# Scatters of the last routing group made independent, and a slot's row load moved behind two weight pieces

## The chip, the cores and the metric

The kernel runs on one core of one Trainium2 chip. The metric is device time in microseconds (us) of one execution. A profile records one execution; its span runs from the first to the last instruction.

## The reference, cut to what matters

Three layers follow each other: a gated linear attention over 4 x 8 heads of 768 steps, a dense feed-forward layer with softplus (3072 tokens, 384 -> 2048 -> 384), and a mixture of eight experts with one expert for each token. The change touches the way from the second to the third layer and the third layer:

```python
def _moe2_ref(x, modality_id, w_gate, modality_bias, w1, w2):
    logits = x @ w_gate + modality_bias[modality_id]
    e_idx = np.argmax(logits, axis=1)
    ...
    gate_w = probs[np.arange(N), e_idx]
    for e in range(E):
        mask = e_idx == e
        h = np.maximum(x[mask] @ w1[e], 0.0)
        out[mask] = gate_w[mask, None] * (h @ w2[e])
```

Here N is 3072, D is 384, E is 8 and the hidden width of an expert is 1024.

## The kernel before, in words

Names used below: PE is TensorE's matmul, ACT is ScalarE, DVE is VectorE, POOL is GpSimd and SP is SyncE, on whose queue nearly all loads are issued.

**Routing.** The 3072 tokens are eight groups of 384. When the feed-forward layer has finished a group, `route1` takes its outputs out of PSUM and `route2` computes each token's expert and its place among that expert's rows (`pos`). Three indirect DMAs from POOL (L492), 128 tokens each, then scatter the rows into `xs`, a buffer in DRAM sorted by expert. A row is 388 floats: 384 values, the gate weight, the token's number and two zeros. All three write the one tensor `xs`, so each waits until the one before has landed. Before the last group's scatters, `pad_rows` (L828, eight DMAs from SP) fills the places behind each expert's rows.

**Slots.** The third layer works in slots: up to 256 rows of one expert (a pair slot) or 128 rows (a single). There are 16: slots 0 to 2 are planned before the last group is routed, their rows are loaded early, and slots 3 to 15 after it (`plan_rest`); slots 3 to 11 are pair slots, slots 12 to 15 are singles. A slot's work is

- `m_load` (L702): SP reads the row offset from the plan (`roff`) and issues one DMA `xr <- xs` (L705). There are three `xr` buffers, so the rows of slot x+1 go into the buffer of slot x-2, whose last reader is the output scatter of slot x-2 (it takes the token numbers from `xr`). That load also waits for the scatters into `xs`.
- `m_weights` (L708): SP reads the expert's number (`woff`); eight pieces of 384 KB follow, w1 and w2 by turns. I number them p0 to p7, so p0, p2, p4, p6 are w1 and p1, p3, p5, p7 are w2. A piece goes into one of six `raw` buffers (L724), ACT rounds it to the high part (L725) and DVE takes the remainder as the low part (L726), which frees the `raw` buffer. In singles w1 goes straight into place (L721). The split weights have two sets of buffers, by turns of slots.
- `m_T` (L730): PE turns the rows (L746, in two steps, four and two transposes), ACT and DVE split them into `thl` (L748, L749). The two steps share one PSUM buffer.
- `m_up` (L751): eight steps of 9 matmuls from `thl` and w1 (L764), each followed by relu on ACT (L766) and a remainder on DVE (L767).
- `m_down` (L780): 24 matmuls for each 128 rows (L787), scaling on ACT into `o` (L791), and an indirect DMA from POOL that scatters the result rows to `out` (L792). All of these write `out`, so each waits until the one before has landed.

**Order.** `m_slots` (L803) runs slot x, and at its start calls `m_fetch` for slot x+1, which before the change calls `m_load` first and `m_weights` after it; the eight pieces are then issued one for each step of `m_up`, and `m_T` of slot x+1 follows step 6. An engine executes its own queue strictly in order. The order within a queue is set when the kernel is built, by a planner that starts from the order of the program and from the dependencies and may move instructions of an engine past each other.

Of the kernel before, what the change touches and what calls it, by code (L numbers as in the profile page):

```python
# [20 lines left out]
TG = 384  # L21
NG = NT // TG
# [3 lines left out]
SLOT = 256  # L26
# [16 lines left out]
RW = 388  # L43
# [7 lines left out]
def moe_chain(ctx, tc, qT, kT, fT, vp, w_in, w_out, mod, w_gate, mbias, w1, w2, out):  # L51
    nc = tc.nc
# [15 lines left out]
    xs = dp.tile([E * CAP + SLOT, RW], F32, name="xs")  # L68
# [173 lines left out]
    padt = cp.tile([128, RW], F32, name="padt")  # L242
# [190 lines left out]
            del gst[s]  # L433


    rt = {}

    def sm(nm, shape, dt=F32):
        return gp.tile(shape, dt, tag=nm, name=nm)
# [12 lines left out]
    def route2(G):  # L452
        d = rt[G]
        lg, rows = d["lg"], d["rows"]
        mx = sm("mx", [128, 3])
        oh = sm("oh", [128, 3, 8])
        sc = sm("sc", [128, 3, 8])
        ohb = sm("ohb", [128, 3, 8], BF16)
        m2 = sm("m2", [128, 3])
        bc = lambda t: t.unsqueeze(2).to_broadcast([128, 3, 8])  # L460
        nc.vector.tensor_reduce(mx, lg, axis=AX.X, op=ALU.max)
        nc.vector.tensor_tensor(oh, lg, bc(mx), op=ALU.is_equal)
        nc.vector.tensor_tensor(sc, oh, wt8.unsqueeze(1).to_broadcast([128, 3, 8]), op=ALU.mult)
        nc.vector.tensor_reduce(m2, sc, axis=AX.X, op=ALU.max)
        nc.vector.tensor_scalar(m2, m2, 1.0, None, op0=ALU.max)
        nc.vector.tensor_tensor(oh, sc, bc(m2), op=ALU.is_equal)
        nc.vector.tensor_copy(ohb, oh)
        p = ps_r.tile([128, 512], F32, tag="r", name="r")
        for j in range(3):
            pj = p[:, 8 * j:8 * j + 8]  # L470
            nc.tensor.matmul(pj, onesb, runb, start=True, stop=False)
            for i in range(j):
                nc.tensor.matmul(pj, onesb, ohb[:, i, :], start=False, stop=False)
            nc.tensor.matmul(pj, ustr, ohb[:, j, :], start=False, stop=True)
        for j in range(3):
            nc.vector.tensor_tensor(run, run, oh[:, j, :], op=ALU.add)
        nc.vector.tensor_copy(runb, run)
        nc.vector.tensor_tensor(sc, p[:, 0:24].rearrange("p (j e) -> p j e", j=3),
                                base.unsqueeze(1).to_broadcast([128, 3, 8]), op=ALU.add)
        nc.vector.tensor_tensor(sc, sc, oh, op=ALU.mult)  # L480
        nc.vector.tensor_reduce(m2, sc, axis=AX.X, op=ALU.add)
        pos = sm("pos", [128, 3], I32)
        nc.vector.tensor_scalar(pos, m2, BIG, None, op0=ALU.add)
        nc.vector.tensor_tensor(lg, lg, bc(mx), op=ALU.subtract)
        nc.scalar.activation(lg, lg, AF.Exp)
        nc.vector.tensor_copy(rows.bitcast(I32)[:, :, 385], ids[:, 3 * G:3 * G + 3])
        nc.vector.memset(rows[:, :, 386:388], 0.0)
        nc.vector.tensor_reduce(mx, lg, axis=AX.X, op=ALU.add)
        nc.vector.tensor_scalar(mx, mx, 1e-9, None, op0=ALU.add)
        nc.vector.reciprocal(rows[:, :, 384], mx)  # L490
        for j in range(3):
            nc.gpsimd.indirect_dma_start(  # L492
                out=xs, out_offset=bass.IndirectOffsetOnAxis(ap=pos[:, j:j + 1], axis=0),
                in_=rows[:, j, :], in_offset=None, bounds_check=E * CAP - 1, oob_is_err=False,
            )
        del rt[G]


# [144 lines left out]
    for u in range(4, 33):  # L643
        G, j = divmod(u, 4)
# [11 lines left out]
    for G in range(NG - 1):  # L656
        at(16 * G + (19 if G in (0, NG - 2) else 23), lambda G=G: route2(G))
# [44 lines left out]
    def m_load(s, roff, i, n):  # L702
        ro = nc.sync.value_load(roff[0:1, i:i + 1], min_val=0, max_val=PADROW)
        xr = xrp.tile([128, 2, RW], F32, tag="xr", name="xr")[:, 0:n, :]
        nc.sync.dma_start(xr, xs[bass.ds(ro, 128 * n), :].rearrange("(p j) w -> p j w", j=n))  # L705
        sl[s] = {"xr": xr, "n": n}

    def m_weights(s, woff, i, whole):  # L708

        wo = nc.sync.value_load(woff[0:1, i:i + 1], min_val=0, max_val=E - 1)  # L710
        pl = m1p[s % 2]
        names = ("w1h", "w1l", "w2h", "w2l")
        w1h, w1l, w2h, w2l = wts[s] = [pl.tile([128, 3 * FE], F32R, tag=n, name=n) for n in names]
        ops = []
        for n in range(4):
            for src, hi, lo in ((w1, w1h, w1l), (w2, w2h, w2l)):
                def op(n=n, src=src, hi=hi, lo=lo):
                    c = slice(768 * n, 768 * n + 768)
                    rows = src[bass.ds(wo, 1), :, c].rearrange("o p f -> p (o f)")
                    if whole and src is w1:  # L720
                        nc.sync.dma_start(hi[:, c].bitcast(F32), rows)  # L721
                        return
                    t = rawp.tile([128, 768], F32, tag="raw", name="raw")
                    nc.sync.dma_start(t, rows)  # L724
                    nc.scalar.copy(hi[:, c], t)  # L725
                    nc.vector.tensor_tensor(lo[:, c], t, hi[:, c].bitcast(F32), op=ALU.subtract)  # L726
                ops.append(op)
        return ops
# [72 lines left out]
    plans = {}  # L801

    def m_slots(items, last):  # L803

        for x, (s, it) in enumerate(items):
            nxt = items[x + 1] if x + 1 < len(items) else None
            wops = []
            if nxt:
                wops = m_fetch(*nxt)
            for f in range(NF2):  # L810
                if f >= ahead or s:
                    m_up(s, f)
                if f == 3 and not s:
                    last()
                if wops:
                    wops.pop(0)()
                if f == 6 and nxt:
                    m_T(nxt[0])
            for j in range(it[2]):
                m_down(s, j)  # L820

    def m_fetch(s, it):
        where, i, n = it
        if s not in sl:
            m_load(s, plans[where][1], i, n)
        return m_weights(s, plans[where][0], i, n == 1)

    def pad_rows(e):  # L828

        r = nc.sync.value_load(plans["first"][2][0:1, e:e + 1], min_val=e * CAP, max_val=e * CAP + NT - TG)  # L830
        nc.sync.dma_start(xs[bass.ds(r, TG + SLOT), :].rearrange("(p j) w -> p j w", j=5),
                          padt.unsqueeze(1).to_broadcast([128, 5, RW]))

    def pre():
        plans["first"] = plan_first()
        for i in range(NPRE):
            m_load(i, plans["first"][1], i, 2)
        for n, op in enumerate(m_fetch(0, seq[0])):
            at(16 * (NG - 1) + PRE + 1 + n, op)
        for e in range(E):  # L840
            at(16 * (NG - 1) + PRE + e, lambda e=e: pad_rows(e))
# [27 lines left out]
    def final():  # L869
        for j in range(3):  # L870
            route1(NG - 1, j)
        route2(NG - 1)
        plans["rest"] = plan_rest()
# [5 lines left out]
    with tc.If(nv > NSTAT):  # L879
        more = [(len(seq) + x, it) for x, it in enumerate(more)]  # L880
        for op in m_fetch(*more[0]):
            op()
        m_T(more[0][0])
        m_slots(more, None)
# [175 lines left out]
```

## Time and profile before

| what | value |
|---|---|
| median of 3 runs | 853.9 us (853.63 to 854.34) |
| profiled execution | 851.32 us, of which the span is 849.3 us |
| PE busy | 807.5 us (95% of the span) |
| DVE, ACT, POOL busy | 648.3, 545.1 and 65.2 us |
| mean granted TensorE clock | 0.987 of full speed |
| matmuls | 5887 |

Matmuls are pipelined and their shown durations overlap, so the pace is read from start to start. "Idle before" in a row is the time in which the engine stood still ahead of that instruction, with the instruction or DMA that ended it; where a wait is for several things the one named is that which came last by the profile.

### The profile page before, as it was taken

How to read it: one execution, taken by the hardware profiler on the slowest of the kernel's cores; microseconds unless marked ns; L12 is line 12 of the kernel's file. 1: busy time of each engine (PE TensorE's matmuls, PEld its weight loads, DVE VectorE, ACT ScalarE, POOL GpSimd, SP SyncE). 2: the span in 40 equal slices, each digit the busy share in tenths (PEclk: the TensorE clock that was granted, in tenths of full speed). 3: DMA queues.
4: the chain of work that ended last, by engine and by line, in shares of the span. 5: the costliest groups of instructions: out<-in, count | busy, mean ns of one | idle time of the engine just before them, and what ended most of it. 6: DMA issues, size and time to landing. Idle time of an engine off the chain costs nothing. (4 is left out here: it accounts for less than half of the span.)

```text
span 849.3 us, 16229 instructions
## 1 busy us (share of the span) xinstructions
PE 807.5 (95%) x5887; PEld 746.6 (88%) x5887; DVE 648.3 (76%) x1325; ACT 545.1 (64%) x1142; POOL 65.2 (8%) x79
## 2 busy tenths in 40 slices
PE   5789999999999999999999999999899999999994
PEld 4545667999999999999999999989899999999984
DVE  7889999988887888888888866888766656555341
ACT  6788766776677776677776655676567555555341
POOL 2000000100010010010010010101211101011000
PEclk9989999999999999999999999999989999999997
DMA  8666221222132122132121000399785667655580
GB/s 284 211 227 190 89 72 55 72 63 65 43 95 61 52 82 65 42 96 60 52 72 47 10 34 8 108 351 327 237 276 204 212 219 260 215 202 187 188 309 15
DMA packets 61854, 115.87 MB, mean 136 GB/s; under 512 B 7976, under 2 KB 39515, under 8 KB 61761
## 3 DMA queue, kind: packets, MB, share of 16 engines
q1 hardware_dynamic: 57472, 104.76, 38.4%
q0 software_dynamic: 3328, 9.49, 3.0%
q8 instruction: 50, 0.82, 0.4%
q10 hardware_dynamic: 960, 0.44, 0.2%
q14 instruction: 44, 0.35, 0.1%
HBM read 92.11 MB, written 18.62 MB: 130 GB/s over the span
## 5 line engine op out<-in xcount | busy, mean ns | idle before, releaser
L352 PE MATMUL h<-xh,wih 128*128 128x384 f32 x336 | 118.3, 352 | 0.9 <-DVE e L366 0.5
L428 PE MATMUL x2ps<-woh,hi 128*128 128x392 f32 x336 | 115.1, 343 | 1.0 <-ACT hi L388 1.0
L428 PE MATMUL x2ps<-woh,lo 128*128 128x392 f32 x336 | 114.8, 342 | 0.4 <-DVE lo L389 0.4
L428 PE MATMUL x2ps<-wol,hi 128*128 128x392 f32 x336 | 114.7, 341 | 0.0
L352 PE MATMUL h<-xh,wil 128*128 128x384 f32 x336 | 112.8, 336 | 0.0
L352 PE MATMUL h<-xl,wih 128*128 128x384 f32 x336 | 112.7, 335 | 0.0
L764 PE MATMUL h<-thl,w1h 128*128 128x256 f32 x576 | 108.0, 288 | 3.7 <-ACT thl L748 3.6
L764 PEld LDWEIGHTS h<-thl,w1h 128*128 128x128 f32 x576 | 91.5, 194 | 4.7 <-ACT thl L748 3.8
L726 DVE TENSOR_TENSOR w2l<-raw,w2h 128x768 fp32r<-128x768 f32 x64 | 60.7, 950 | 35.2 <-ACT w2h L725 35.1
L764 PE MATMUL h<-thl,w1l 128*128 128x256 f32 x288 | 81.6, 285 | 0.0
L726 DVE TENSOR_TENSOR w1l<-raw,w1h 128x768 fp32r<-128x768 f32 x48 | 45.7, 954 | 46.0 <-ACT w1h L725 45.0
L787 PE MATMUL x2ps<-w2h,hl 128*128 128x384 f32 x224 | 75.8, 339 | 1.9 <-DVE hl L767 1.0
L787 PE MATMUL x2ps<-w2h,hh 128*128 128x384 f32 x224 | 77.0, 344 | 0.4 <-ACT hh L766 0.4
L725 ACT CAST w1h<-raw 128x768 fp32r<-128x768 f32 x48 | 40.1, 835 | 57.9 <-DMA raw<-in_w_dram 57.3
L414 ACT CAST hi<-l 128x768 fp32r<-128x768 f32 x48 | 39.9, 832 | 56.5 <-DVE l L413 41.7
L787 PE MATMUL x2ps<-w2l,hh 128*128 128x384 f32 x224 | 75.0, 336 | 0.0
L492 POOL DMA_INDIRECT xs<-rows,pos x24 | 28.8, 1201 | 565.2 <-DVE F L110 149.8
L352 PEld LDWEIGHTS h<-xh,wih 128*128 128x128 f32 x336 | 63.1, 188 | 4.7 <-DVE e L366 1.3
L428 PEld LDWEIGHTS x2ps<-woh,hi 128*128 128x128 f32 x336 | 63.1, 188 | 2.0 <-ACT hi L388 1.9
L428 PEld LDWEIGHTS x2ps<-woh,lo 128*128 128x128 f32 x336 | 63.1, 188 | 1.2 <-DVE lo L389 1.0
L352 PEld LDWEIGHTS h<-xl,wih 128*128 128x128 f32 x336 | 63.2, 188 | 0.3 <-DVE xl L226 0.3
L428 PEld LDWEIGHTS x2ps<-wol,hi 128*128 128x128 f32 x336 | 63.1, 188 | 0.0
(203 smaller groups left out, 1868.0 us busy)
## 6 DMA issues: line engine op xcount, KB each, us to landing
raw<-in_w_dram SPq DMA_DIRECT2D x112, 384.0 KB
xs<-padt SPq DMA_DIRECT2D x8, 970.0 KB
f<-in_f_dram SPq DMA_DIRECT2D x32, 192.0 KB
k<-in_k_dram SPq DMA_DIRECT2D x32, 192.0 KB
q<-in_q_dram SPq DMA_DIRECT2D x32, 192.0 KB
st<-in_w_in_dram SPq DMA_DIRECT2D x16, 384.0 KB
st<-in_w_out_dram SPq DMA_DIRECT2D x16, 384.0 KB
w1h<-in_w_dram SPq DMA_DIRECT2D x16, 384.0 KB
```

Of the source, the lines that this page charges most:

```text
L352: nc.tensor.matmul(hp, w, x, start=(n == 0), stop=(n == len(terms) - 1))
L414: nc.scalar.copy(hi, g)
L428: nc.tensor.matmul(x2ps[j][:, 0:DM + 8], g[:, ts], w, start=(i == 0 and n == 0), stop=(i == NF - 1 and n == len(terms) - 1))
L492: nc.gpsimd.indirect_dma_start(out=xs, out_offset=bass.IndirectOffsetOnAxis(ap=pos[:, j:j + 1], axis=0), in_=rows[:, j, :], in_offset=None ...
L725: nc.scalar.copy(hi[:, c], t)
L726: nc.vector.tensor_tensor(lo[:, c], t, hi[:, c].bitcast(F32), op=ALU.subtract)
L764: nc.tensor.matmul(hp[:, 0:SLOT], w[:, kd, fs], t[:, x, kd, :], start=(n == 0), stop=(n == 8))
L787: nc.tensor.matmul(acc[:, 0:DM], g[:, f, ts], w[:, f, :], start=(f == 0 and n == 0), stop=(f == NF2 - 1 and n == 2))
```

## The change

1. The three scatters of the last group (G = 7) no longer wait for each other: the dependency between them is declared away, and each waits for the eight pad DMAs itself (before, the second and third had this through the first).
2. `m_load` of a slot from 3 on waits explicitly for all three scatters.
3. In `m_fetch`, `m_load` moves: it no longer stands ahead of the slot's eight weight pieces, but is called just before the third (p2), so p0 and p1 are issued first.

```diff
+    rt, scat, pads = {}, [], []
+    def after(ins, other):
+        tc.add_manual_dep(ins, other.name, ..., reason="rows of the buffer")
...
         for j in range(3):
-            nc.gpsimd.indirect_dma_start(
+            ins = nc.gpsimd.indirect_dma_start(
                 out=xs, ...
+            ).ins
+            if G == NG - 1:
+                for other in scat:
+                    tc.declare_no_dep(ins, other, reason="rows of different tokens")
+                for pad in pads:
+                    after(ins, pad)
+                scat.append(ins)
...
     def m_load(s, roff, i, n):
-        nc.sync.dma_start(xr, xs[bass.ds(ro, 128 * n), :]...)
+        ins = nc.sync.dma_start(xr, xs[bass.ds(ro, 128 * n), :]...).ins
+        for other in scat:
+            after(ins, other)
...
     def m_fetch(s, it):
         where, i, n = it
+        ops = m_weights(s, plans[where][0], i, n == 1)
         if s not in sl:
-            m_load(s, plans[where][1], i, n)
-        return m_weights(s, plans[where][0], i, n == 1)
+            op = ops[2]
+            ops[2] = lambda: (m_load(s, plans[where][1], i, n), op())
+        return ops
...
     def pad_rows(e):
-        nc.sync.dma_start(xs[bass.ds(r, TG + SLOT), :]...)
+        pads.append(nc.sync.dma_start(xs[bass.ds(r, TG + SLOT), :]...).ins)
```

## Rows read from the trace of the kernel before

**Rows 1.** Busy time by stretch: slot 2, slot 3, slots 8 and 9, slot 12, slots 13 and 14.
```profile
612.05:637.00 24.95, 21.03 (x128) 20.05 (x127) 14.22 (x22) 13.54 (x25) 3.24 (x3) 0.86 0.84 277
637.00:654.45 17.45, 17.45 (x127) 17.32 (x127) 11.17 (x18) 11.30 (x21) 2.59 (x3) 1.00 0.67 237
724.86:762.22 37.36, 36.25 (x254) 35.00 (x254) 21.89 (x37) 20.90 (x40) 4.09 (x4) 1.00 0.62 212
797.04:806.90 9.86, 9.86 (x77) 9.86 (x77) 4.98 (x8) 5.25 (x10) 1.03 (x1) 1.00 0.44 150
806.90:828.52 21.62, 20.70 (x151) 19.48 (x151) 9.47 (x16) 10.82 (x20) 1.95 (x2) 1.00 0.85 303
```

**Rows 2.** Timeline of PE around the start of slot 2 (start, duration, instruction, idle before).
```profile
610.08 0.38 PE L746 MATMUL r<-ident,xr 128*128 128x128 f32 x2
...
612.64 0.28 PE L764 MATMUL h<-thl,w1l 128*128 128x256 f32 x1
616.48 1.04 PE L764 MATMUL h<-thl,w1h 128*128 128x256 f32 x2 [3.57 <-ACT thl L748]
...
622.41 0.28 PE L764 MATMUL h<-thl,w1l 128*128 128x256 f32 x1
...
626.12 0.60 PE L746 MATMUL r<-ident,xr 128*128 128x128 f32 x4
```

**Rows 3.** Busy time by stretch, two microseconds behind that gap; the column behind POOL is the granted clock.
```profile
618.00:620.00 2.00, 2.00 (x11) 2.00 (x11) 0.96 (x1) 2.00 (x5) 0.60 (x1) 0.50 1.04 295
```

**Rows 4.** Timeline of ACT ahead of the same gap.
```profile
595.06 0.57 ACT L791 ACTIVATE o<-x2ps,xr 128x384 f32<-128x384 f32 x1
...
607.52 0.37 ACT L766 ACTIVATE hh<-h 128x256 fp32r<-128x256 f32 x1
615.33 0.83 ACT L725 CAST w1h<-raw 128x768 fp32r<-128x768 f32 x1 [7.44 <-DMA raw<-in_w_dram]
616.07 0.36 ACT L748 CAST thl<-r 128x256 fp32r<-128x256 f32 x1
```

**Rows 5.** Timeline of SP's queue, from slot 0's last weights to slot 3's.
```profile
579.56 23.35 SPq L724 DMA_DIRECT2D raw<-in_w_dram  x17
609.50 0.34 SPq L705 DMA_DIRECT2D xr<-xs  x1
610.72 9.17 SPq L724 DMA_DIRECT2D raw<-in_w_dram  x8
```

**Rows 6.** Timeline of POOL: the last group's scatters and slot 0's two output scatters.
```profile
584.63 0.98 POOL L492 DMA_INDIRECT xs<-rows,pos  x1 [44.31 <-DMA raw<-in_w_dram]
591.81 1.80 POOL L492 DMA_INDIRECT xs<-rows,pos  x1 [6.21 <-DMA xs<-rows,pos]
598.18 1.42 POOL L492 DMA_INDIRECT xs<-rows,pos  x1 [4.57 <-ACT w1h L725]
599.90 1.64 POOL L792 DMA_INDIRECT out_dram<-o,xr  x1 [0.31 <-issue]
606.03 1.38 POOL L792 DMA_INDIRECT out_dram<-o,xr  x1 [4.49 <-DMA out_dram<-o,xr]
```

**Rows 7.** Timeline of DVE: first and last of slot 2's last six weight remainders, and `thl`.
```profile
603.22 0.94 DVE L726 TENSOR_TENSOR w1l<-raw,w1h 128x768 fp32r<-128x768 f32 x1
...
608.89 0.67 DVE L749 TENSOR_TENSOR thl<-r,thl 128x512 fp32r<-128x512 f32 x1
...
609.82 0.94 DVE L726 TENSOR_TENSOR w2l<-raw,w2h 128x768 fp32r<-128x768 f32 x1
```

**Rows 8.** The output scatters' line, all 28: time from issue to landing.
```profile
DMA to landing us min/median/max: 2.4/2.7/7.2
```

**Rows 9.** Timeline of SP's queue: the row load of slot 11, during slot 9.
```profile
750.23 0.33 SPq L705 DMA_DIRECT2D xr<-xs  x1
```

**Rows 10.** Timeline of ACT: the first and the last w1 piece of slot 11.
```profile
755.21 0.83 ACT L725 CAST w1h<-raw 128x768 fp32r<-128x768 f32 x1 [2.59 <-DMA raw<-in_w_dram]
...
762.91 0.83 ACT L725 CAST w1h<-raw 128x768 fp32r<-128x768 f32 x1 [0.58 <-DMA raw<-in_w_dram]
```

More of the change, by code (lines that the diff above doesn't have):

```diff
@@ L433, in down @@
             del gst[s]
-    rt = {}
+    rt, scat, pads = {}, [], []
+    def after(ins, other):
+        tc.add_manual_dep(ins, other.name, mybir.DependencyInfo(mybir.DependencyClass.Sync, mybir.DependencyReason.DATA),
+                          reason="rows of the buffer")
     def sm(nm, shape, dt=F32):
@@ L491, in route2 @@
         for j in range(3):
-            nc.gpsimd.indirect_dma_start(
+            ins = nc.gpsimd.indirect_dma_start(
                 out=xs, out_offset=bass.IndirectOffsetOnAxis(ap=pos[:, j:j + 1], axis=0),
                 in_=rows[:, j, :], in_offset=None, bounds_check=E * CAP - 1, oob_is_err=False,
-            )
+            ).ins
[5 more added lines that the diff above has]
+                scat.append(ins)
         del rt[G]
@@ L704, in m_load @@
         xr = xrp.tile([128, 2, RW], F32, tag="xr", name="xr")[:, 0:n, :]
-        nc.sync.dma_start(xr, xs[bass.ds(ro, 128 * n), :].rearrange("(p j) w -> p j w", j=n))
+        ins = nc.sync.dma_start(xr, xs[bass.ds(ro, 128 * n), :].rearrange("(p j) w -> p j w", j=n)).ins
+        for other in scat:
+            after(ins, other)
         sl[s] = {"xr": xr, "n": n}
@@ L823, in m_fetch @@
         where, i, n = it
+        ops = m_weights(s, plans[where][0], i, n == 1)
         if s not in sl:
-            m_load(s, plans[where][1], i, n)
-        return m_weights(s, plans[where][0], i, n == 1)
+            op = ops[2]
+            ops[2] = lambda: (m_load(s, plans[where][1], i, n), op())
+        return ops
     def pad_rows(e):
         r = nc.sync.value_load(plans["first"][2][0:1, e:e + 1], min_val=e * CAP, max_val=e * CAP + NT - TG)
-        nc.sync.dma_start(xs[bass.ds(r, TG + SLOT), :].rearrange("(p j) w -> p j w", j=5),
-                          padt.unsqueeze(1).to_broadcast([128, 5, RW]))
+        pads.append(nc.sync.dma_start(xs[bass.ds(r, TG + SLOT), :].rearrange("(p j) w -> p j w", j=5),
+                                      padt.unsqueeze(1).to_broadcast([128, 5, RW])).ins)
     def pre():
```

## The prediction, made before the changed kernel was run

> **What bounds the kernel now.** I read the share of each engine first, then the third layer slot by slot, then the queues backward from the one place where PE stands still. PE is the bound: in slot 3 it is busy in all of 17.45 us, and DVE and ACT in 11 each [rows 1]. So an edit counts only where PE waits. The largest such place is slot 2, which takes 24.95 us for the same work, at a mean clock of 0.86 [rows 1]. Two things lie in it. PE starts a matmul at 612.64, and the next at 616.48, after 3.57 us idle, waiting for ACT's `thl` [rows 2]. And behind the gap the granted clock is 0.50, TensorE's lower level of 1.2 GHz [rows 3]: the matmuls from 616.48 up to 622.41 run at half pace [rows 2].
>
> Who is late? ACT. Its `thl` cast at 616.07 takes 0.36 us and had its input since the transposes of 610.08 [rows 2, 4]. But ahead of it in ACT's queue stands p0 of slot 3, which found no data until 615.33; ACT stood idle 7.44 us for it [rows 4]. Who kept p0? SP. It issued slot 2's last piece at 602.91 (579.56 + 23.35) and then nothing until the row load of slot 3 at 609.50; p0 follows at 610.72 and is cast 4.61 us later [rows 4, 5]. So the queue stood still for 6.59 us at the row load, and behind it stood weights that did not need it.
>
> What did the row load wait for? The three scatters into `xs`, and slot 0's two output scatters, which free its buffer. POOL issues the five at 584.63, 591.81, 598.18, 599.90 and 606.03, each held by the landing of another [rows 6]; the last is issued at 606.03, ends at 607.41 and has to land before 609.50.
>
> **The change part by part.** *Scatters made independent.* The first is held as before, by its places and by the pads. The second and third have nothing left to wait for: the places of all three come from one instruction and the pads are done. At 0.98 to 1.80 us each on POOL [rows 6] the third ends near 584.63 + 0.98 + 1.80 + 1.42 + two gaps of about 0.3 (the gap between the third and the next, 0.31) = 589.4 instead of 599.60. Slot 0's first output is then free of the queue; its data come from two ACT instructions, the later of which ends at 595.63 [rows 4]. It can go near 595 instead of 599.90, and the second one, which still waits for the first to land, 6.13 us later as before (599.90 to 606.03 [rows 6]): near 601 instead of 606. The row load can then go near 605 instead of 609.50. The other end: if landings stay as slow as the slowest, 7.2 us [rows 8], twice in a row, it goes near 609.5 and the scatters bring nothing by themselves. I take 606. By itself this edit is worth nothing but an earlier SP; what it feeds is the next one.
>
> *Row load behind p1.* SP gets to p0 at 602.91. p0 needs a `raw` buffer: the six in use are freed by the last six remainders on DVE, the first of which ends at 603.22 + 0.94 = 604.16, the last at 610.76 [rows 7]. So p0 goes at 604.3 and p1 about 1.3 us later (six buffers in 6.60 us), both ahead of the row load whatever the scatters do. With the 4.61 us that p0 took before, behind a row load and beside five other pieces, it is there by 608.9, and its cast, 0.83 us, ends by 609.8. The transposes that `thl` needs are at 610.08 and end at 610.46, so `thl` is cast by about 610.9, 1.9 us before PE is through the six matmuls that do without it (612.76). The stall goes whole, with 1.9 us to spare, even if p0 is as slow as before. These transposes themselves are not moved: they wait for DVE's 608.89 + 0.67 to give back the PSUM buffer [rows 7].
>
> What is late next? p2 to p7 stand behind the row load. With the row load at 606, p2 goes near 606.8 (when its `raw` buffer is free, by the same pace) and is there by 611.4; with the row load at 609.50, near 614.7. The second would hold ACT, and with it slot 2's relus, until 614.7, while PE has four PSUM buffers of ups to fill: 4 x 9 x 0.12 = 4.3 us from 612.05, so until 616.3. That cover is enough. Slot 3's rows are needed only at step 6 of slot 2, seven steps of 1.08 us behind 612.05, so 619.6: over 9 us behind the latest row load.
>
> *The sum for slot 2.* Gap: 616.48 - 612.64 - 0.12 = 3.72 us. Clock: from 616.48 to 622.41 PE starts 26 matmuls in 5.93 us; from 622.41 to 626.12 it starts 31 in 3.71 us [rows 2], 0.120 each; so 26 would take 3.11, and 2.82 come back. Together 6.54 us. The other bound is slot 3's length: 24.95 - 17.45 = 7.50 [rows 1]. I take 7.0.
>
> *The other slots.* In each, p0 and p1 now go before SP waits for the output of slot x-2. For slot 11 the row load stood until 750.23, and p0 was cast at 755.21 after ACT had waited 2.59 us for it [rows 9, 10]. Such waits hold a relu or an output behind them, and slots 8 and 9 took 37.36 us against 2 x 17.45: at most 2.46 us to gain. Slots 13 and 14 took 21.62 against 2 x 9.86 of slot 12: at most 1.90 [rows 1]. Below, nothing. I take half of the first, 1.2, since slot 3 in the same order has no gap, and a quarter of the second, 0.5, since there the DMA engines are busy 0.85 of the time and an earlier issue only starts them earlier.
>
> *What costs nothing.* The three added waits of each row load and the pad waits of each scatter are for transfers that landed long before, except in slot 3; SP and POOL have room for them, as PE waits for neither. If that cover went (SP late by the wait), the price would be that of the last rival. The moved read of `roff` costs SP the same in either place, under 0.9 us (from 609.84 to 610.72 [rows 5] SP reads `woff` and waits for nothing else).
>
> The sum: 7.0 + 1.2 + 0.5 = 8.7 us. From the profiled execution's 851.32 that gives 842.6. The median of the runs, 853.9, lies 2.6 above it, so I predict 845.2.
>
> **The rivals.** *A part of the stall stays.* The planner may put another piece ahead of `thl` in ACT's queue, for instance p2. It then depends on the row load: with 606 there is no stall, with 609.5 p2 is cast by 615.5, and PE waits until about 615.9, nearly as before. In between, a stall of 1 to 3 us with half pace behind it leaves a gain of some 2 us: 852. For it: ACT's order has a piece ahead of `thl` already [rows 4]. Against: p0 must come first, and p2's buffer is not late.
>
> *The change does not do what it says.* Both landings stay slow and p2 is ahead of `thl`, or the planner restores the old order on SP: 853.9.
>
> *Slower: outputs land later.* p0 and p1 are now in flight while slot x-2's last output lands, which the row load, and with it p2 to p7, waits for. Output scatters took 2.4 to 7.2 us to land, 2.7 in the median [rows 8]. For slot 11, nine transfers (a row load of 388 KB and eight pieces of 384) took from 750.23 to 762.91, 12.7 us; the seven that remain behind the wait carry 2692 of 3460 KB, so at this pace 9.9 us. The row load may slip by 2.8 us before the last w1 piece is later than now, and that piece is cast at 762.91, 0.7 us behind the slot's start. A slip of the full 4.5 us (7.2 - 2.7) makes it 1.7 us late, in some ten slots 17 us, less the 8.7 gained: 862. It decides from a slip of 3.7 us on, where ten times 0.9 eats the gain. Against it: p0 and p1 go as soon as a buffer is free, mostly before that output is issued. The Trainium skill, DMA: Bandwidth & Descriptors, Issuing engines are not separate DMA queues, speaks for this rival: transfers of all engines run on the same 16 DMA engines and interleave. The trace agrees so far as its slowest landings are more than twice the median.
>
> **How the numbers follow.** The forecast, stall gone, 0.73: 845.2, its own range 842.0 (7.50 + 2.46 + 1.90 gained) to 847.4 (6.54 alone). A part stays, 0.12: 848 to 852. No effect, 0.05: 853.9. Slower, 0.10: 856 to 862. Faster by over 0.2%, that is 1.7 us, about what can be told from no change: 0.73 + 0.12 = 0.85; within 0.2%: 0.05; slower: 0.10. The range goes from 842.0 to 852.0: it leaves out the last two cases, 0.15, and a little for a pace outside my bounds.
>
> **What would show it.** Right: the second and third scatter about 1 to 2 us behind the first; two L724 issues ahead of L705 in SP's queue, the first near 604; ACT's `thl` near 611; no PE gap over 1 us at slot 2, no clock of 0.50 behind it, and slot 2 near 17.5 us. Wrong: a gap of PE with `thl` behind another piece, output landings near 7 us in all slots, or slots longer than 17.7.

## The result, and the profile after

The changed kernel takes 843.49 us in the median of 5 runs (841.77 to 844.21), the kernel before 853.63 us (850.89 to 854.34) beside it: a ratio of 0.9906, interval 0.9885 to 0.9927. Measured again beside some of the experiments it was 0.9919 (0.9891 to 0.9946; 843.22 against 850.87 us). So it is faster by 0.8 to 0.9%, some 8 to 10 us; 845.2 was forecast.

The span fell from 849.3 to 840.8 us. I divide it at the starts of slots: the first up matmul behind the last down matmul of the slot before (slot 1: 594.52 before and 594.00 after; later ones in the windows below).

| stretch | before | after | difference |
|---|---|---|---|
| up to slot 1 | 594.52 | 594.00 | -0.52 |
| slot 1 | 17.53 | 18.66 | +1.13 |
| slot 2 | 24.95 | 17.89 | -7.06 |
| slots 3 to 11 | 160.04 | 159.94 | -0.10 |
| slots 12 to 15, to the last matmul's start | 40.85 | 39.12 | -1.73 |
| from there to the end of the span | 11.41 | 11.19 | -0.22 |

Busy time by stretch of the changed kernel, for slots 1, 2, 3, for 5 and 6 together, for 3 to 11 and for 12 to 15 (columns as in [rows 1]: the stretch and its length, the busy us of PE, of its weight loads, of DVE, ACT and POOL, each with a count, then the granted clock, the share of DMA and GB/s):

```profile
594.00:612.66 18.66, 17.95 (x127) 17.38 (x127) 17.55 (x38) 13.26 (x24) 2.80 (x3) 1.00 0.94 305
612.66:630.55 17.89, 17.82 (x127) 17.51 (x127) 12.50 (x21) 11.43 (x22) 1.97 (x2) 1.00 0.85 272
630.55:648.05 17.50, 17.50 (x127) 17.36 (x127) 10.95 (x19) 10.46 (x20) 2.47 (x2) 1.00 0.72 222
665.80:703.25 37.45, 36.18 (x253) 35.22 (x253) 23.27 (x37) 22.08 (x43) 5.90 (x5) 1.00 0.69 216
630.55:790.49 159.94, 158.67 (x1132) 156.82 (x1132) 93.66 (x154) 89.51 (x172) 20.89 (x19) 1.00 0.68 214
790.49:829.61 39.12, 39.12 (x297) 38.90 (x297) 17.11 (x28) 18.26 (x35) 4.70 (x4) 1.00 0.60 212
```

The gap at slot 2 and the half clock behind it are gone: the clock is 1.00 in all of slot 2, where it was 0.86 on average [rows 1]. Slots 3 to 11 cost what they did, but the two slow ones are now 5 and 6 (37.45 us) where they were 8 and 9.

The queues that led to the gap, after. POOL's timeline, against [rows 6]:

```profile
583.50 0.97 POOL L496 DMA_INDIRECT xs<-rows,pos  x1 [44.28 <-DVE nsl L589]
584.78 0.97 POOL L496 DMA_INDIRECT xs<-rows,pos  x1 [0.30 <-issue]
586.07 1.50 POOL L496 DMA_INDIRECT xs<-rows,pos  x1 [0.30 <-issue]
594.17 1.43 POOL L805 DMA_INDIRECT out_dram<-o,xr  x1 [6.61 <-ACT o L804]
600.46 1.03 POOL L805 DMA_INDIRECT out_dram<-o,xr  x1 [4.85 <-ACT thl L761]
```

The second and third scatter follow 0.30 us behind the one before, and the first output waits for its data alone. SP's queue, against [rows 5]; the count of 19 in the first row is two more than before, p0 and p1 of slot 3, which stand alone, at 603.93 and 604.99, in two narrower views of the same queue under it:

```profile
578.44 26.88 SPq L737 DMA_DIRECT2D raw<-in_w_dram  x19
606.30 0.33 SPq L716 DMA_DIRECT2D xr<-xs  x1
606.89 10.55 SPq L737 DMA_DIRECT2D raw<-in_w_dram  x8
```

```profile
603.93 0.34 SPq L737 DMA_DIRECT2D raw<-in_w_dram  x1
604.99 0.33 SPq L737 DMA_DIRECT2D raw<-in_w_dram  x1
```

ACT's timeline, against [rows 4]: the first row is the last piece of slot 2, the third p0 of slot 3.

```profile
608.00 0.83 ACT L738 CAST w2h<-raw 128x768 fp32r<-128x768 f32 x1 [2.43 <-DMA raw<-in_w_dram]
608.74 0.38 ACT L779 ACTIVATE hh<-h 128x256 fp32r<-128x256 f32 x1
609.02 0.83 ACT L738 CAST w1h<-raw 128x768 fp32r<-128x768 f32 x1
611.11 0.37 ACT L761 CAST thl<-r 128x256 fp32r<-128x256 f32 x1 [1.26 <-PE r L759]
```

The order is that of before, p0 ahead of `thl`, but p0 is there, and ACT waits for PE's transposes, not for a transfer. Most of what slot 1 lost, 0.71 of 1.13 us, is the first row: its last relu stands behind a piece of slot 2 that came late, and PE waits 0.71 us for it. In the second profile of this kernel slot 1 took 17.50 us, so this is not in every execution.

What did not come is a gain in the other pair slots. Two things got worse beside it: the landing of the output scatters, and the place of the row loads. The landings, and the row loads in slots 4 and 5, after and then before:

```profile
DMA to landing us min/median/max: 2.2/4.3/7.2
```

```profile
656.73 0.33 SPq L716 DMA_DIRECT2D xr<-xs  x1
...
675.33 0.33 SPq L716 DMA_DIRECT2D xr<-xs  x1
```

```profile
659.60 0.33 SPq L705 DMA_DIRECT2D xr<-xs  x1
...
677.22 0.33 SPq L705 DMA_DIRECT2D xr<-xs  x1
```

The median landing rose from 2.7 [rows 8] to 4.3 us, and the row loads stand 8.7 and 9.5 us behind the starts of slots 4 and 5 (648.05 and 665.80), where they stood 5.2 and 5.1 us behind them before (654.45 and 672.09). The Trainium skill, DMA: Bandwidth & Descriptors, Issuing engines are not separate DMA queues, has transfers of all engines interleave on the same DMA engines. The runs below fit that: the median landing is 2.7 us with the scatters alone and 4.1 with the row load alone, where weights go out ahead of the wait; that the weights are what slows it is not shown apart. Nor do these rows say that a late row load costs time: what the pair slots wait for is settled by the experiments.

### The profile page after: what moved, and what is told of

It reads as the page before. It is cut to its first block, busy times and chain, and to the rows that moved or that the text cites. A ratio compares the mean times of both kernels' runs of the same rounds, so it can differ in the third digit from the quotient of the medians.

```text
span 840.8 us, 16231 instructions
## 1 busy us (share of the span) xinstructions
PE 804.6 (96%) x5887; PEld 745.7 (89%) x5887; DVE 647.8 (77%) x1325; ACT 546.2 (65%) x1142; POOL 65.1 (8%) x79
## 5 line engine op out<-in xcount | busy, mean ns | idle before, releaser
L777 PE MATMUL h<-thl,w1h 128*128 128x256 f32 x576 | 105.7, 284 | 1.3 <-DVE hl L780 1.3
L777 PEld LDWEIGHTS h<-thl,w1h 128*128 128x128 f32 x576 | 89.2, 189 | 2.3 <-DVE hl L780 1.7
```

The costliest lines, as they stand in the source:

```text
L777: nc.tensor.matmul(hp[:, 0:SLOT], w[:, kd, fs], t[:, x, kd, :], start=(n == 0), stop=(n == 8))
```

## The experiments

All times below are medians of five to twelve executions; ratios are to the kernel before, measured beside it on the same chip. The slots, in us, are those of one profiled execution of each run, which can lie some us from the median: 849.82 for the scatters alone and 852.05 for slot 3's row load alone, 2.4 and 3.0 above their medians.

| run | median us | ratio (interval) | slot 1 | slot 2 | slots 3-11 | 12-15 |
|---|---|---|---|---|---|---|
| before | | 1 | 17.53 | 24.95 | 160.04 | 40.85 |
| the change | 843.49 | 0.9906 (0.9885-0.9927) | 18.66 | 17.89 | 159.94 | 39.12 |
| the change again | 843.22 | 0.9919 (0.9891-0.9946) | 17.50 | 18.72 | 158.82 | 39.53 |
| scatters only | 847.42 | 0.9953 (0.9935-0.9972) | 18.30 | 20.42 | 159.95 | 42.89 |
| row load only | 842.18 | 0.9906 (0.9882-0.9930) | 17.53 | 20.80 | 159.77 | 38.94 |
| slot 3's row load only | 849.02 | 0.9968 (0.9947-0.9988) | 18.05 | 21.79 | 163.45 | 39.92 |
| same, outputs independent | 843.87 | 0.9918 (0.9891-0.9946) | 17.54 | 19.39 | 159.84 | 39.49 |
| change, behind p0 | 849.50 | 0.9989 (0.9967-1.0010) | 18.16 | 17.99 | 167.50 | 39.17 |
| behind p0, outputs independent | 841.85 | 0.9881 (0.9853-0.9908) | 17.69 | 19.13 | 157.43 | 40.23 |
| change, outputs independent | 840.19 | 0.9879 (0.9850-0.9907) | 17.52 | 19.20 | 157.70 | 38.93 |
| change, behind p5 | 841.09 | 0.9888 (0.9866-0.9910) | 18.10 | 18.04 | 157.41 | 40.82 |
| behind p5 in pairs, p1 in singles | 838.12 | 0.9857 (0.9828-0.9886) | 17.54 | 18.31 | 157.64 | 39.21 |
| same, outputs independent | 840.92 | 0.9880 (0.9852-0.9907) | 17.53 | 19.16 | 157.66 | 38.94 |
| same, scatters chained again | 839.91 | 0.9871 (0.9844-0.9898) | 17.53 | 18.47 | 157.42 | 38.94 |

**The two halves of the change, each alone.** Scatters independent, row load where it was:

```diff
     def m_fetch(s, it):
         where, i, n = it
+        if s not in sl:
+            m_load(s, plans[where][1], i, n)
+        return m_weights(s, plans[where][0], i, n == 1)
```

> The scatters of the last group independent, the row load left ahead of all eight pieces. Theory A (the stall in slot 2 is p0 of slot 3 held back in SP's queue by the row load; whatever lets SP go on early cures it): the second output of slot 0 lands about 5 us earlier, the row load goes near 605 instead of 609.5, p0 is cast near 610 to 611 and the stall in slot 2 is under 1 us: about 7 us faster than before, 846 to 848, without the 1.7 us that the singles gained. Theory B (only the place of the row load counts): the stall stays at 3.6 us, 852 to 854.

The row load alone: the kernel before with the new `m_fetch` and nothing else.

> The row load behind p1, the three scatters chained as before. Theory A: p0 and p1 go near 604 and 605, the row load near 609.5; p2 is late, but ACT has the cast of thl ahead of it, so the stall in slot 2 is gone: 843 to 846. Theory C (the gain comes from rows and outputs of slot 0 that are earlier): the stall stays, 852 to 854.

Either half takes away the stall of 3.57 us, so theories B and C fall. With the scatters alone the row load goes at 606.73 and p0 is cast at 612.22, before slot 2 starts at 613.89; slot 2 is 4.5 us shorter, and no gap of PE in it is over 0.9 us. The median lies in the range that was expected, but only 3.2 us under the kernel before, where 7 were expected; in the profile slot 3 took 19.94 us and a single slot 13.82, where the kernel before has 17.45 and 9.86 to 10.90. With the row load alone PE stands idle in slot 2 three times for 0.73 to 0.83 us, and the slot takes 20.80 us; in slots 3 to 15 it is as good as the whole change, and the ratio is the same, 0.9906. ACT's timeline of that run shows the cause of the first gap, PE's the gap:

```profile
608.04 0.37 ACT L748 CAST thl<-r 128x256 fp32r<-128x256 f32 x1 [1.46 <-PE r L746]
608.39 0.58 ACT L791 ACTIVATE o<-x2ps,xr 128x384 f32<-128x384 f32 x1
612.01 0.83 ACT L725 CAST w1h<-raw 128x768 fp32r<-128x768 f32 x1 [3.03 <-DMA raw<-in_w_dram]
612.75 0.58 ACT L791 ACTIVATE o<-x2ps,xr 128x384 f32<-128x384 f32 x1
613.22 0.82 ACT L725 CAST w2h<-raw 128x768 fp32r<-128x768 f32 x1
613.94 0.39 ACT L766 ACTIVATE hh<-h 128x256 fp32r<-128x256 f32 x1
```

```profile
614.84 0.50 PE L764 MATMUL h<-thl,w1h 128*128 128x256 f32 x2 [0.79 <-DVE hl L767]
```

`thl` is in time, but ACT waits for p2, behind the row load of 607.30, and behind p2 stand an output, a w2 piece and only then the first relu of slot 2.

**The stall by itself.** Only slot 3's row load is moved, the scatters stay chained:

```diff
-        if s not in sl:
+        if s not in sl and s != 3:
             m_load(s, plans[where][1], i, n)
-        return m_weights(s, plans[where][0], i, n == 1)
+        ops = m_weights(s, plans[where][0], i, n == 1)
+        if s == 3:
+            op = ops[2]
+            ops[2] = lambda: (m_load(s, plans[where][1], i, n), op())
+        return ops
```

> The kernel before with one thing changed: slot 3's row load stands behind p1; all other row loads and the chained scatters are as before. Theory A (p0 of slot 3 held back ahead of thl in ACT's queue makes the stall in slot 2): the stall of 3.6 us and the half clock behind it go, slots 1 and 2 take about 38.5 us together instead of 42.5, as in the run with the move alone; slots 3 to 15 stay as before: 4 us less than before, 846 to 848. If the stall has another cause: 850 to 851.

The orders of ACT and PE are those of the kernel before; on SP one row load stands two pieces later. Slots 1, 2, and 4 to 11 by stretch:

```profile
596.59:614.64 18.05, 17.78 (x128) 17.29 (x127) 17.33 (x38) 12.69 (x23) 4.88 (x4) 1.00 0.78 256
614.64:636.43 21.79, 18.90 (x128) 17.64 (x128) 12.62 (x21) 11.83 (x22) 1.96 (x2) 1.00 0.82 280
655.63:799.88 144.25, 142.29 (x1007) 139.47 (x1006) 81.77 (x135) 78.12 (x151) 16.89 (x16) 1.00 0.61 208
```

No gap over 1.1 us, and the clock is 1.00: theory A holds for the stall. But slots 1 and 2 gave back 2.64 us, less than the 4 expected, and slots 3 to 11 took 3.41 more, 1.75 of them in slot 3 (19.20 us) and 1.66 in slots 4 to 11 (144.25 against 142.59). In this execution the time saved in slot 2 was lost later, in slots where nothing was edited; by the medians 2.6 us are left (0.9968), and 849.02 misses the 846 to 848 that was expected. Something other than PE sets the pace there.

**Where the row load stands.** The change with the row load behind p0, then behind p5:

```diff
-            op = ops[2]
-            ops[2] = lambda: (m_load(s, plans[where][1], i, n), op())
+            op = ops[1]          # behind p0;  ops[6]: behind p5
+            ops[1] = lambda: (m_load(s, plans[where][1], i, n), op())
```

> As the change, but the row load behind p0 only. Theory D (p1's wait for a raw buffer and its traffic beside the output scatters hold the row load back, by 3 us in slots 3 to 8, which brings the gaps of slots 5 and 6): the row load goes 1 to 3 us earlier after a slot's start than with the change, the two gaps of 0.6 us shrink, and slots 3 to 11 take 1 to 2 us less: 841.5 to 843. If p1 is not the cause: 843 to 844, and the row load as late as with the change.

> As the change, but the row load behind p5. Theory E (the row load's wait for slot x-2's output holds p2 and p4, ACT waits for p4 ahead of the output of the slot before, so the outputs and with them the next row load are late): p2 and p4 are cast 2 us or more earlier, slots 3 to 11 take about 17.45 each, 157.5 in all instead of 159.9: 841 to 842. If rows become late instead: gaps of PE at the transposes of a slot, and 845 or more.

Theory D is wrong: one piece fewer ahead made slots 3 to 11 7.6 us longer than the change, and slots 5 to 10 take 18.9 to 19.3 us each. Theory E holds: behind p5 they take 157.41 us. That an even 18.9 us returns slot after slot points to a ring of waits. Once around, in the run behind p0: SP's queue with two row loads, then ACT's timeline, then POOL's, between them.

```profile
693.19 0.33 SPq L716 DMA_DIRECT2D xr<-xs  x1
...
712.17 0.33 SPq L716 DMA_DIRECT2D xr<-xs  x1
```

```profile
700.22 0.83 ACT L738 CAST w1h<-raw 128x768 fp32r<-128x768 f32 x1 [5.07 <-DMA raw<-in_w_dram]
702.19 0.83 ACT L738 CAST w1h<-raw 128x768 fp32r<-128x768 f32 x1 [1.14 <-DMA raw<-in_w_dram]
702.93 0.58 ACT L804 ACTIVATE o<-x2ps,xr 128x384 f32<-128x384 f32 x1
...
704.84 0.57 ACT L804 ACTIVATE o<-x2ps,xr 128x384 f32<-128x384 f32 x1
```

```profile
703.78 1.08 POOL L805 DMA_INDIRECT out_dram<-o,xr  x1 [12.31 <-ACT o L804]
709.21 1.17 POOL L805 DMA_INDIRECT out_dram<-o,xr  x1 [4.34 <-ACT hh L779]
```

The row load of slot 8 goes at 693.19, during slot 6, and p1 to p7 behind it. p2 and p4 are cast when they land, at 700.22 and 702.19, and only behind p4 stands the first output of slot 6, 702.93. POOL scatters it at 703.78. The second output is there at 705.41 (704.84 + 0.57), but its scatter goes at 709.21, 5.43 us behind the first: as in [rows 6], it waits for the landing of the first, and the ACT instruction that the row names is not its data. SP waits for the landing of that, as slot 9 takes the buffer of slot 6, and the next row load goes at 712.17: 18.98 us once around, where PE needs 17.45 for a slot. The row loads of the kernel before stand 17.49, 18.64, 18.56 and 18.52 us apart from 695.54 to 768.75 (the fourth of these five is that of [rows 9]), around the slow slots 8 and 9. That fits the same ring, which eats the lead of the weights until a slot or two are late; in the kernel before it is argued from these spacings alone. In the change the spacings are 17.28 to 18.60 us from 621.71 to 692.89, and 17.16 and less behind that, up to 743.51.

**Breaking the ring.** If that is so, it is broken where the two output scatters wait for one another, with the row load left at the worst place:

```diff
-    rt, scat, pads = {}, [], []
+    rt, scat, pads, outs = {}, [], [], []
...
-        nc.gpsimd.indirect_dma_start(
+        ins = nc.gpsimd.indirect_dma_start(
             out=out, out_offset=bass.IndirectOffsetOnAxis(ap=xr.bitcast(I32)[:, j, 385:386], axis=0),
             in_=o, in_offset=None, bounds_check=NT - 1, oob_is_err=False,
-        )
+        ).ins
+        for other in outs:
+            tc.declare_no_dep(ins, other, reason="rows of different tokens")
+        outs.append(ins)
```

> The row load behind p0, as in the run where pair slots took 18.9 us, and in addition the output scatters independent of each other (they write rows of different tokens). Theory F (a ring of waits sets those slots: row load, then p4, which ACT casts ahead of the first output, then the first output scatter, then the second, which waits for the first to land, then the next row load; 18.98 us around, more than PE's 17.45): without the wait between the two output scatters the ring is 2.5 to 4 us shorter, PE is the bound again, slots 5 to 11 take 17.5 each: about 9 us less than with the row load behind p0 alone, 840 to 843. If it is the order of the weights that PE or DVE cannot follow: 18.9 us as before, 848 to 850.

Slots 3 to 11 with the ring closed (the first row, the run behind p0), and broken:

```profile
628.14:795.64 167.50, 161.66 (x1132) 157.76 (x1132) 93.88 (x154) 89.43 (x173) 22.35 (x19) 1.00 0.63 205
```

```profile
632.84:790.27 157.43, 157.43 (x1132) 156.40 (x1132) 93.41 (x153) 90.40 (x172) 18.60 (x19) 1.00 0.67 216
```

PE is busy in every one of the 157.43 us, with the same weights and row loads in the same order. Its POOL timeline has the second scatter as soon as its data are there, and its row loads follow PE's pace (689.18 and 706.91, 17.73 apart):

```profile
699.97 0.98 POOL L805 DMA_INDIRECT out_dram<-o,xr  x1 [12.51 <-ACT o L804]
704.13 0.98 POOL L805 DMA_INDIRECT out_dram<-o,xr  x1 [3.19 <-ACT o L804]
```

So theory F is shown for the row load behind p0: the wait of the second output scatter for the first, in a ring with the row load and the weights behind it, set the pace of the pair slots. The same edit on the change as it is, and the change once more beside it:

> The changed kernel, and the output scatters independent of each other. Theory F: the gaps of slots 5 and 6 go, slots 3 to 11 take 157.5 instead of 159.9: 2 us less than the changed kernel in the same call. If the ring is not what makes these gaps: no difference.

> The changed kernel once more, as the base for the others on this chip: 841 to 844, 0.9% under the kernel before.

Slots 3 to 11 fall to 157.70 us, 2.2 below the first profile of the change and 1.1 below the second; the ratios, 0.9879 and 0.9919, point the same way, but their intervals touch. In the second profile of the change no slot stands out as 5 and 6 did; slot 3 has the gap (18.86 us), and slot 1 has none. Where the lead runs out differs from one execution to the next. On the run with only slot 3's row load moved, the edit should have brought slots 3 to 11 to 157.5 us:

> The run with slot 3's row load alone moved, and the output scatters independent of each other; row loads of slots 4 to 15 still ahead of all their weights. There slots 3 to 11 took 163.4 us, 3.4 more than before, and ate most of what slot 2 gave back. Theory F (the ring row load, p4, output, output, row load is the bound of those slots once PE is earlier): without the wait between outputs slots 3 to 11 take 157.5 us, 841 to 844. If the earlier PE meets another bound there (weights that arrive late because eight pieces follow the row load): 160 us or more, 847 to 849.

```profile
651.74:791.72 139.98, 139.98 (x1007) 139.06 (x1007) 82.15 (x135) 79.41 (x151) 16.07 (x16) 1.00 0.63 216
```

```profile
644.75 0.83 ACT L725 CAST w1h<-raw 128x768 fp32r<-128x768 f32 x1 [3.68 <-DMA raw<-in_w_dram]
```

Slots 4 to 11, above, took 139.98 us instead of 144.25 (142.59 in the kernel before), so what was lost there was the ring. But slot 3 took 19.86 us (19.20 without the edit), and 3 to 11 together took 159.84. The ACT row shows what slot 3 waited for: p0 of slot 5, behind that slot's row load of 639.36, held ACT for 3.68 us and slot 3's relus behind it. That is the form of the old stall, p0 behind a row load, and it stays with the outputs independent; so the 1.75 us that slot 3 lost above are not shown to be the wait between outputs. The time of 843.87 lies in the expected range, the slots do not.

**A better version.** The row load behind p5 opens the ring too: p2 and p4, which held the first output in ACT's queue, go ahead of it, and ACT casts them there without a wait (690.55, in one slot). In singles it was too late there: a row load landed late, and PE stood idle 1.70 us for it in a slot that took 11.76 us. So behind p5 in pairs, and where the change has it in singles:

```diff
-            op = ops[2]
-            ops[2] = lambda: (m_load(s, plans[where][1], i, n), op())
+            k = 6 if n == 2 else 2
+            op = ops[k]
+            ops[k] = lambda: (m_load(s, plans[where][1], i, n), op())
```

> The row load behind p5 in pair slots, where all slots took 17.5, and behind p1 in singles, where a row load behind p5 made PE wait 1.7 us. Both theories: that gap goes, 1.5 to 2 us less than with the row load behind p5 everywhere: 3 to 4 us less than the changed kernel in the same call, 838 to 840.

838.12 us, 0.9857 (0.9828 to 0.9886), against 0.9919 (0.9891 to 0.9946) for the change measured beside it. The intervals don't overlap: it beats both kernels. Slots 3 to 11 stand at PE's pace, and the clock is whole:

```profile
627.36:785.00 157.64, 157.64 (x1132) 156.47 (x1132) 92.49 (x153) 89.42 (x172) 17.93 (x18) 1.00 0.67 216
```

Then both ways out of the ring together, and the same with the three scatters into `xs` chained again as in the kernel before:

> The row load behind p5 in pair slots and behind p1 in singles, the scatters into xs independent as in the change, and the output scatters independent too: both ways out of the ring together. Theory F: the ring is not the bound any more with either, so little is added to the row load behind p5: 0 to 1 us less, 837 to 839.

> As the run with the row load behind p5 in pair slots and the output scatters independent, but the three scatters into xs chained again. It prices the scatters' edit where nothing else holds. Theory A: slot 3's row load goes about 3 us later, p6 and p7 of slot 3 behind it; w1's other pieces are ahead, so under 1.5 us: 838 to 840. If the scatters' independence is worth more by itself: 841 or more.

0.9880 and 0.9871: neither can be told from the other or from 0.9857, and 840.92 us is above the 837 to 839 expected of the first. One way out of the ring is enough. And once the row load stands behind p5 in the pair slots and the outputs are independent, whether the three scatters wait for one another makes no difference that these runs can measure.

## Why the prediction was right or wrong

The forecast of 845.2 us was 1.7 above the time, within its range. The sum behind it was 8.7 us of gain; the spans of the profiled executions differ by 8.5, the medians by 10.1 in the first measurement and 7.7 in the second. The stall of slot 2, most of the sum, came as the prediction had it. But two terms had another size, and something else lay beneath one of them.

- **The scatters.** Right: the third was to end near 589.4 and ended at 587.57; slot 0's outputs were to go near 595 and 601 and went at 594.17 and 600.46; the row load near 606, and it went at 606.30. (Not each of the five was held by a landing before: the first output followed the third scatter by 0.31 us [rows 6].) "By itself this edit is worth nothing but an earlier SP" was wrong: alone it gives 0.47%, since the earlier SP lets p0 come early enough for the stall of 3.57 us to go. With the move made, it is worth nothing that the times show (0.9906 with it and without it), though the profile has slots 1 and 2 at 36.55 us with it and 38.33 without.
- **The row load behind p1.** Right: p0 was to go at 604.3 and went at 603.93, p1 1.06 us behind it; `thl` was to be cast by 610.9 and was at 611.11, before PE ran out.
- **The sum for slot 2.** Right: 7.0 us was taken, 7.06 came, and no clock of 0.50 is left. In the second profile of the change slot 2 took 18.72 us, 6.23 less than before. Slot 1 lost 1.13 us in the first and nothing in the second.
- **"That cover is enough".** Wrong, and hidden by the scatters. With the row load alone, that load went at 607.30, 2.29 us ahead of slot 2's start at 609.59, about where the late case of the prediction had it (609.50, 2.55 ahead of 612.05). p2 was there 2.42 us behind the start, no later than the 2.65 of that case. But the prediction stopped at p2: behind it an output and a w2 piece came first, the first relu began only at 613.94, and PE could go on at 614.84, 5.25 us behind the start, where four PSUM buffers were to last 4.3. Slot 2 took 20.80 us.
- **"I take half of the first, 1.2" (pair slots).** The size is not settled: 0.10 in the profile of the change, 1.22 in its second one. That the second fits is luck: the half was a choice, taken from the wait of p0 in one slot, which was not followed round. The outputs land later, as the slower rival had it (median 4.3 instead of 2.7 us), and the row loads in slots 4 and 5 stood 3.5 and 4.4 us further behind the slot's start than in the same slots before, beyond the 2.8 us that the rival allowed (it counts p7 as landed by 762.91, where [rows 10] show the cast of p6 alone) and around the 3.7 where it was to decide. Slots 5 and 6 took 18.64 and 18.81 us, above the 17.7 that the prediction named as a sign of being wrong, but others got shorter, and the 17 us of the rival did not come. Beneath both lies the ring, which no term of mine has: with it broken, 2.3 to 2.6 us come (157.70 to 157.43), the whole bound of 2.46.
- **"A quarter of the second, 0.5" (singles and the end).** Mis-sized: 1.73 us in the first profile and 1.32 in the second, against the bound of 1.90. The reason given, that at 0.85 of the DMA engines' time an earlier issue helps little, is not borne out, nor is the contrary shown: slots 12 to 15 took 38.93 to 39.53 us in the seven profiles with the row load of the singles behind p1, and 39.49 to 42.89 in the four with it ahead of all weights, the kernel before among them. The spread of the latter is larger than the term.
- **What costs nothing.** Right: the added waits cost nothing that a row shows.

The 1.2 us that the singles brought beyond the forecast pay for the 1.1 that the pair slots lacked, and 0.74 at the two ends of the span for most of what slot 1 lost: the forecast is closer than its terms.

## What to carry to other kernels

A transfer that has to wait holds all that stands behind it in its issuing queue (here SP stood still for 6.59 us [rows 5]); put what doesn't need the wait ahead of it, and look for the latest place where its own data still come in time (here, of the places tried, behind p5 of eight for pairs and p1 for singles). Where removing a stall gives less than its size, compare the spacing of a periodic transfer with the period of the bound: if they are close, follow its wait once around, through buffer, cast, output and landing, until it comes back to itself, and cut the ring at the cheapest wait, here one scatter waiting for another that writes other rows.

## What the runs showed of the hardware that was not expected

The same output scatter of 128 rows took 2.2 to 7.2 us to land in the change; its median in a run went from 2.7 to 4.3 us with no edit to it, once the row load stood behind p1.

The clock does not follow the length of one idle stretch alone. In the run with the scatters only, PE stood idle in a single slot for 1.41 us and, soon behind it, for 0.42 us (until 812.43 and 813.48), and the clock then fell; in the stretch shown its mean lies between full speed and the lower level of 0.50, or 1.2 GHz:

```profile
814.00:816.00 2.00, 2.00 (x9) 2.00 (x8) 1.29 (x2) 1.58 (x4) 0.00 (x0) 0.59 0.97 306
```

In the run behind p5 one idle stretch of 1.70 us, until 802.09, left it whole, and so did one of 1.41 us, until 623.73, in the run of slot 3's row load with the outputs independent. The stretch behind the 1.70 us:

```profile
802.00:808.00 6.00, 5.91 (x40) 5.94 (x41) 2.25 (x3) 2.98 (x6) 0.27 (x1) 1.00 0.97 308
```

PE's start of slot 1 came between 591.5 and 596.6 us in kernels and executions that hardly differ up to there. So I compared stretches, not spans.
